# Feature-map attention and two feed-forward stages: the first key block in two transfers, and constants on other queues and places

## The chip, the cores and the metric

The kernel runs on one core of a Trainium2 chip. The metric is the device time of one execution in microseconds (us). Engines are named as in the profile: PE is TensorE, PEld its weight loads, DVE is VectorE, ACT is ScalarE, POOL is GpSimd, SP is SyncE. A name with a q behind it (SPq, ACTq) is that engine's queue of DMA issues.

## The reference

```python
# q, k, v: (4, 8, 576, 64); omega: (128, 64); x = attention output as (2304, 512)
def phi(x):                      # of q * scale and k * scale
    proj = einsum('bhsd,md->bhsm', x, omega)
    h = proj - sum(x * x, -1, keepdims=True) / 2
    return exp(h - max(h, -1, keepdims=True)) / sqrt(m)
kv, z = einsum('bhsm,bhsd->bhmd', phi(k), v), sum(phi(k), 2)
attn = einsum('bhsm,bhmd->bhsd', phi(q), kv) / (einsum('bhsm,bhm->bhs', phi(q), z) + 1e-6)
# then: top-1 mixture of 8 experts (relu, 512 -> 1024 -> 512), gate-weighted,
# then: h = x @ w_in (512 -> 2048), g = piecewise-quadratic relu of h, out = g @ w_out
```

## The kernel before

The program has three stages. The **attention stage** takes the first 172 us; the **expert stage** gathers each expert's tokens and multiplies them by split float32 weights; the **last stage** is the dense layer pair. The last two are nearly back-to-back matmuls on PE.

In the attention stage each head's keys and queries come in blocks of 256 tokens (8 heads, 128 partitions, two tokens to a partition: 512 KB) and in small blocks of the 64 tokens left over in each of two batches. `block_tasks` (L418) makes the work of a block: its load (issued on SP, L432, or L428 for a small one), the squares (ACT for keys, L438; POOL for queries, L440), a tree of two additions on POOL (L445), and a sum on DVE (L449) that gives the squared norm. `unit_tasks` (L465) makes the work of half a block, a unit: four transposes on PE against the identity (L472), a copy on ACT (`th`, L477), 32 small matmuls against omega (`project`, L484), two maxima on DVE (L491), the bias from the maxima and the norm (L495 and L496), and eight exponentials on ACT (L500). The units go k(0,0) first half, the small key block, k(0,1) first half, k(0,0) second half, k(0,1) second half, and then the keys of the next batch and the queries of this one in turn. `kv_tasks`, `c_tasks` and `r_tasks` (L518, L571, L644) come behind: the key-value products, the quotient, and the routing to experts.

Tasks are not run in the order in which they are written. `Plan` (L40) holds them with an engine, a cost in ns, a rank, the tasks they come after and the buffers that they take; `run` picks greedily, by planned start and rank, and then emits all of them in the order of their planned starts. The engines run their own instructions strictly in that order. The planned costs only set the order, never a time on the chip. A load is taken to be usable 2000 ns behind its planned end (`HOPS`, L53). A DMA that is issued outside a task stands in front of all planned work of its engine.

The constants lie in one array of 708 columns: the identity (128 columns, 64 KB), and behind it a triangle of ones, a ramp, token numbers and others (580 columns, 290 KB). The tile is `cs`; the identity is loaded at L191 outside the plan. `omega_tasks` (L382) holds one SP task with three DMAs (omega twice, L387, 32 KB each; the rest of `cs`, L388), the cast of the triangle to bf16 on DVE (`trib`, L397), the transpose of omega on PE (L391), and its scaled copy on ACT (`oms`, L394), which every `project` needs.

The gate's weights are spread into a block matrix by two DVE copies (`gate_blocks`, L413), and four weight tiles of the first expert are loaded and split inside the plan (L281 on POOL, L290 on DVE).

Of the kernel before, what the change touches and what calls it, by code (L numbers as in the profile page):

```python
# [8 lines left out]
F32 = mybir.dt.float32  # L9
# [6 lines left out]
AX = mybir.AxisListType.X  # L16
# [3 lines left out]
P = 128  # L20
B, H, S, HD = 4, 8, 576, 64
# [18 lines left out]
class Plan:  # L40
# [22 lines left out]
    def add(self, engine, cost, fn, rank, after=(), take=(), use=(), mode=None):  # L63
        for b in use:
            b["uses"] += 1
        self.tasks.append((engine, cost, fn, rank, [a for a in after if a is not None], take, use, mode))
        return len(self.tasks) - 1
# [94 lines left out]
def kernel(  # L162
# [14 lines left out]
    nc = tc.nc  # L177
# [10 lines left out]


    cs = cp.tile([P, C_END], F32, name="cs")  # L190
    nc.sync.dma_start(out=cs[:, 0:P], in_=consts[:, 0:P])  # L191
    ident = cs[:, C_ID:C_ID + P]
    trib = cp.tile([P, P], BF16, name="trib")
    oneb = cp.tile([P, P], BF16, name="oneb")
# [129 lines left out]
    with ExitStack() as actx:  # L324
        ap = actx.enter_context(tc.tile_pool(name="ap", bufs=2))
# [19 lines left out]
        add, buf, at = plan.add, plan.buf, plan.tile  # L345
# [33 lines left out]
        om2 = ac.tile([P, 2 * HD], F32, name="om2")  # L379
        oms = ac.tile([P, P], F32, name="oms")  # L380

        def omega_tasks():  # L382
            pb = buf("ps")

            def load():
                for i in range(2):
                    nc.sync.dma_start(out=om2[:, i * HD:(i + 1) * HD], in_=omega)  # L387
                nc.sync.dma_start(out=cs[:, P:C_END], in_=consts[:, P:C_END])  # L388

            def turn():  # L390
                nc.tensor.transpose(at(pb)[:, 0, :], om2, ident)  # L391

            def scaled():
                nc.scalar.activation(oms, at(pb)[:, 0, :], AF.Copy, scale=SCALE)  # L394

            def tri():
                nc.vector.tensor_copy(trib, cs[:, C_TRI:C_TRI + P])  # L397

            x = add("SP", 1300, load, -7.5)
            add("DVE", 130, tri, 1, after=[x])  # L400
            x = add("PE", 110, turn, -5, after=[x], take=[pb], mode="whole")
            return add("ACT", 240, scaled, -5, after=[x], use=[pb])

        wgr = ac.tile([P, 4, E], F32, name="wgr")
# [13 lines left out]
        def block_tasks(which, blk, rank):  # L418
            src = q if which == "q" else k
            small = blk[0] == "s"  # L420
            n = H if small else 2 * H
            o = {"buf": buf("blk")}

            def load():
                t = at(o["buf"])
                if small:
                    for i in range(2):
                        nc.sync.dma_start(out=t[64 * i:64 * i + 64, 0:H, :],  # L428
                                          in_=src[2 * blk[1] + i, :, 512:576, :].rearrange("h p d -> p h d"))
                else:  # L430
                    b, i = blk
                    nc.sync.dma_start(out=t.rearrange("p (h r) d -> p h r d", r=2),  # L432
                                      in_=src[b, :, i * 256:(i + 1) * 256, :].rearrange("h (p r) d -> p h r d", r=2))

            def square(eng):
                raw, t = at(o["buf"])[:, 0:n, :], at(sb)[:, 0:n, :]
                if eng == "ACT":
                    act.activation(t, raw, AF.Square)  # L438
                else:
                    pool.tensor_mul(t, raw, raw)  # L440

            def tree():
                t = at(sb)[:, 0:n, :]
                for w in (32, 16):
                    pool.tensor_add(t[:, :, 0:w], t[:, :, 0:w], t[:, :, w:2 * w])  # L445

            def total():
                o["nsq"] = ap.tile([P, 2 * H], F32, name="nsq", tag="nsq", bufs=12)
                dve.reduce_sum(o["nsq"][:, 0:n], at(sb)[:, 0:n, 0:16], axis=AX)  # L449

            f = 0.5 if small else 1.0
            sb = buf("sqt")
            o["load"] = add("SP", 2250 * f, load, rank - 8, take=[o["buf"]])
            if which == "k":
                t = add("ACT", 950 * f, lambda: square("ACT"), rank - 0.5, after=[o["load"]], take=[sb], use=[o["buf"]])
            else:
                t = add("POOL", 1900 * f, lambda: square("POOL"), rank - 0.5, after=[o["load"]], take=[sb],
                        use=[o["buf"]])
            t = add("POOL", 2000 * f, tree, rank - 0.4, after=[t], use=[sb])
            o["sq"] = add("DVE", 60 + 270 * f, total, rank - 0.3, after=[t], use=[sb])  # L460
            return o

        def unit_tasks(u, o, rank, prev):  # L465
            which, blk, hf = u
            r = {}
# [32 lines left out]
                    act.activation(at(ppb)[:, 2 * j + i, :], at(pjb[i])[:, j, :], AF.Exp, bias=r["bi"][:, i, j:j + 1])  # L500

            pjb = [buf("ps"), buf("ps")]
            ta = add("PE", 435, turn, rank - 1.5, after=[o["load"]] + prev, take=[ptb], use=[o["buf"], ptb], mode="whole")
            x = add("ACT", 480, copy, rank - 2.4, after=[ta], take=[thb], use=[ptb])
            for c in range(4):
                x = add("PE", 220, lambda c=c: project(c), rank + 1 + 0.1 * c, after=[x, setup],
# [1 line left out]
            ends, tb, t = [], x, x  # L508
            for i in range(2):
                t = add("DVE", 600, lambda i=i: top(i), rank + 4.5, after=[t], use=[pjb[i]])  # L510
            t = add("DVE", 150, bias, rank + 1, after=[t, o["sq"]])
            for i in range(2):
                ends.append(add("ACT", 1005, lambda i=i: exps(i), rank + 2, after=[t] + ends[0:1],
                                take=[ppb] if i == 0 else [], use=[pjb[i]]))
# [798 lines left out]
```

## Time and profile before

| | us |
|---|---|
| median of 3 runs | 829.54 (827.75 to 830.61) |
| the profiled execution, its own time | 828.41 |
| its span, first to last instruction | 826.2 |

| engine | busy us | share of the span |
|---|---|---|
| PE | 778.4 | 94% |
| PEld | 710.1 | 86% |
| DVE | 570.1 | 69% |
| POOL | 388.2 | 47% |
| ACT | 366.9 | 44% |

The shares are means over stages with different limits. The time that a change in one stage is worth is read in that stage. The 2.2 us between the profiled execution's own time and its span lie outside the instructions.

### The profile page before, as it was taken

How to read it: one execution, taken by the hardware profiler on the slowest of the kernel's cores; microseconds unless marked ns; L12 is line 12 of the kernel's file. 1: busy time of each engine (PE TensorE's matmuls, PEld its weight loads, DVE VectorE, ACT ScalarE, POOL GpSimd, SP SyncE). 2: the span in 40 equal slices, each digit the busy share in tenths (PEclk: the TensorE clock that was granted, in tenths of full speed). 3: DMA queues.
4: the chain of work that ended last, by engine and by line, in shares of the span. 5: the costliest groups of instructions: out<-in, count | busy, mean ns of one | idle time of the engine just before them, and what ended most of it. 6: DMA issues, size and time to landing. Idle time of an engine off the chain costs nothing.

```text
span 826.2 us, 16881 instructions
## 1 busy us (share of the span) xinstructions
PE 778.4 (94%) x6530; PEld 710.1 (86%) x6530; DVE 570.1 (69%) x1124; ACT 366.9 (44%) x906; POOL 388.2 (47%) x385
## 2 busy tenths in 40 slices
PE   6798799769999999989999999999999999999996
PEld 4687688649999999979998989898999989898985
DVE  5679888865756876475688667687777877745543
ACT  6798799614422222222354554444433443434331
POOL 5627861444446455163655444453434544334333
PEclk9999999969999999999999999999999999999999
DMA  9958301155465655664432001110011100001112
GB/s 224 225 122 210 116 29 28 54 159 177 155 187 177 191 184 186 114 215 144 141 94 80 27 27 47 56 52 27 28 51 51 52 27 1 1 25 52 40 39 81
DMA packets 79034, 80.41 MB, mean 97 GB/s; under 512 B 28972, under 2 KB 61868, under 8 KB 78944
## 3 DMA queue, kind: packets, MB, share of 16 engines
q1 hardware_dynamic: 75056, 68.10, 29.2%
q0 software_dynamic: 3072, 9.57, 3.3%
q10 hardware_dynamic: 816, 1.57, 0.5%
q8 instruction: 53, 0.87, 0.4%
q14 instruction: 37, 0.30, 0.1%
HBM read 69.78 MB, written 9.45 MB: 96 GB/s over the span
## 4 chain that ended last, share of the span: by engine, by line
PE 71%; DVE 11%; DMA 8%; ACT 4%; issue 3%; POOL 2%; POOLq 0%; SPq 0%; DVEq 0%
PE ph L1117 7%; PE ph L1118 7%; PE ph L1119 7%; PE po L1163 7%; PE po L1162 7%; PE po L1161 7%; DMA out_dram<-acc,oidx 5%; PE py L1031 4%; PE py L1033 3%; PE py L1032 3%; PE ph L1013 3%; PE ph L1014 3%; PE ph L1015 3%; ACT pp L500 3%; DMA wraw<-in_moe_w_dram 2%
## 5 line engine op out<-in xcount | busy, mean ns | idle before, releaser
L1146 POOL TENSOR_TENSOR gl<-cl,gh 128x384 fp32r<-128x384 f32 x94 | 99.5, 1078 | 186.5 <-ACT gh L1145 186.5
L1138 ACT ACTIVATE cl<-cl,half 128x384 f32<-128x384 f32 x96 | 57.0, 615 | 212.4 <-DVE cl L1137 212.4
L1117 PE MATMUL ph<-yh,wh 128*128 128x384 f32 x384 | 129.8, 338 | 0.0
L1118 PE MATMUL ph<-yl,wh 128*128 128x384 f32 x384 | 129.7, 338 | 0.0
L1119 PE MATMUL ph<-yh,wl 128*128 128x384 f32 x384 | 129.7, 338 | 0.0
L281 POOL TENSOR_SCALAR wh<-wraw 128x1024 fp32r<-128x1024 f32 x60 | 75.0, 1252 | 111.9 <-DMA wraw<-in_moe_w_dram 46.8
L1163 PE MATMUL po<-wh,gl 128*128 128x512 f32 x288 | 113.9, 395 | 0.0
L1162 PE MATMUL po<-wl,gh 128*128 128x512 f32 x288 | 113.7, 395 | 0.0
L1161 PE MATMUL po<-wh,gh 128*128 128x512 f32 x288 | 113.6, 394 | 0.0
L1137 DVE TENSOR_SCALAR cl<-ph 128x384 f32<-128x384 f32 x96 | 51.4, 552 | 81.9 <-PE ph L1119 81.1
L290 DVE TENSOR_TENSOR wl<-wraw,wh 128x1024 fp32r<-128x1024 f32 x60 | 77.3, 1288 | 16.3 <-POOL wh L281 16.3
L500 ACT ACTIVATE pp<-ps,bi 128x128 f32<-128x128 f32 x288 | 84.3, 478 | 6.4 <-DVE bi L496 6.4
L937 DVE TENSOR_TENSOR yl<-yT,yh 128x384 fp32r<-128x384 f32 x96 | 79.0, 880 | 8.9 <-ACT yh L936 8.9
L1013 PE MATMUL ph<-xh,wh 128*128 128x288 f32 (+6 forms) x256 | 78.8, 308 | 3.0 <-DVE hl L1019 2.6
L1031 PE MATMUL py<-hh,wh 128*128 128x288 f32 (+6 forms) x256 | 79.1, 309 | 0.0
L1014 PE MATMUL ph<-xl,wh 128*128 128x288 f32 (+6 forms) x256 | 77.2, 302 | 1.1 <-DVE xl L975 1.0
L1032 PE MATMUL py<-hl,wh 128*128 128x288 f32 (+6 forms) x256 | 76.6, 299 | 0.7 <-DVE hl L1019 0.5
L1015 PE MATMUL ph<-xh,wl 128*128 128x288 f32 (+6 forms) x256 | 77.1, 301 | 0.0
L1033 PE MATMUL py<-hh,wl 128*128 128x288 f32 (+6 forms) x256 | 76.6, 299 | 0.4 <-DVE wl L290 0.4
L1117 PEld LDWEIGHTS ph<-yh,wh 128*128 128x128 f32 x384 | 72.1, 188 | 2.1
L1118 PEld LDWEIGHTS ph<-yl,wh 128*128 128x128 f32 x384 | 72.1, 188 | 2.0
L1119 PEld LDWEIGHTS ph<-yh,wl 128*128 128x128 f32 x384 | 72.1, 188 | 0.0
(163 smaller groups left out, 1664.6 us busy)
## 6 DMA issues: line engine op xcount, KB each, us to landing
wraw<-in_moe_w_dram SPq DMA_DIRECT2D x57, 512.0 KB, 3.8
wraw<-in_moe_w_in_dram SPq DMA_DIRECT2D x16, 512.0 KB, 3.9
wraw<-in_moe_w_out_dram SPq DMA_DIRECT2D x16, 512.0 KB, 3.4
blk<-in_k_dram SPq DMA_DIRECT2D x8, 512.0 KB, 6.6
blk<-in_q_dram SPq DMA_DIRECT2D x8, 512.0 KB, 6.1
vm<-in_v_dram SPq DMA_DIRECT2D x16, 256.0 KB, 5.3
xd<-xr SPq DMA_DIRECT2D x16, 256.0 KB, 2.2
wra<-in_moe_w_dram SPq DMA_DIRECT2D x4, 512.0 KB, 7.0
```

The lines of the kernel that those rows point to most:

```text
L500: act.activation(at(ppb)[:, 2 * j + i, :], at(pjb[i])[:, j, :], AF.Exp, bias=r["bi"][:, i, j:j + 1])
L1013: nc.tensor.matmul(ph, lhsT=wh[:, d, c], rhs=xh, start=(d == 0), stop=False)
L1014: nc.tensor.matmul(ph, lhsT=wh[:, d, c], rhs=xl, start=False, stop=False)
L1015: nc.tensor.matmul(ph, lhsT=wl[:, d, c], rhs=xh, start=False, stop=(d == 3))
L1031: nc.tensor.matmul(py, lhsT=wh[:, a, c], rhs=hh, start=(f == 0), stop=False)
L1032: nc.tensor.matmul(py, lhsT=wh[:, a, c], rhs=hl, start=False, stop=False)
L1117: nc.tensor.matmul(ph[f], lhsT=wh[:, a, c], rhs=yh, start=(d == 0), stop=False)
L1118: nc.tensor.matmul(ph[f], lhsT=wh[:, a, c], rhs=yl, start=False, stop=False)
L1119: nc.tensor.matmul(ph[f], lhsT=wl[:, a, c], rhs=yh, start=False, stop=(d == 3))
L1161: nc.tensor.matmul(po, lhsT=gh[:, c], rhs=wh[:, a, :], start=(f == 0), stop=False)
L1162: nc.tensor.matmul(po, lhsT=gh[:, c], rhs=wl[:, a, :], start=False, stop=False)
L1163: nc.tensor.matmul(po, lhsT=gl[:, c], rhs=wh[:, a, :], start=False, stop=(f == 3))
```

## The change

The identity is loaded on ACT's queue in place of SP's. The two omega transfers leave the SP task and are issued on ACT's queue ahead of the plan, behind the identity. The SP task of `omega_tasks` keeps only the 290 KB of other constants; its planned cost goes from 1300 to 600 and its rank from -7.5 to -5.5, and the transpose of omega no longer comes after it. The loads of k(0,0), the small key block and k(0,1) have the ranks -8, -7 and -6. The block k(0,0) alone gets two loads of four heads each (ranks -8 and -7.8), and its squares, tree and sum are made by half; each unit waits only for its own half. All other blocks keep one part.

```diff
-    nc.sync.dma_start(out=cs[:, 0:P], in_=consts[:, 0:P])
+    nc.scalar.dma_start(out=cs[:, 0:P], in_=consts[:, 0:P])
...
+            for i in range(2):
+                nc.scalar.dma_start(out=om2[:, i * HD:(i + 1) * HD], in_=omega)
+
             def load():
-                for i in range(2):
-                    nc.sync.dma_start(out=om2[:, i * HD:(i + 1) * HD], in_=omega)
                 nc.sync.dma_start(out=cs[:, P:C_END], in_=consts[:, P:C_END])
...
-            x = add("SP", 1300, load, -7.5)
+            x = add("SP", 600, load, -5.5)
             add("DVE", 130, tri, 1, after=[x])
-            x = add("PE", 110, turn, -5, after=[x], take=[pb], mode="whole")
+            x = add("PE", 110, turn, -5, take=[pb], mode="whole")
...
+            parts = 2 if which == "k" and blk == (0, 0) else 1
+            w = n // parts
...
+                    h = H // parts
+                    nc.sync.dma_start(out=t[:, i * w:(i + 1) * w, :].rearrange("p (h r) d -> p h r d", r=2),
+                                      in_=src[b, i * h:(i + 1) * h, j * 256:(j + 1) * 256, :].rearrange(
+                                          "h (p r) d -> p h r d", r=2))
...
-            f = 0.5 if small else 1.0
+            f = w / 16
             sb = buf("sqt")
+            o["load"], o["sq"] = [], []
+            for i in range(parts):
+                o["load"].append(add("SP", 2250 * f, lambda i=i: load(i), rank - 8 + 0.2 * i, take=[] if i else [o["buf"]]))
+            for i in range(parts):
+                if which == "k":
+                    t = add("ACT", 950 * f, lambda i=i: square("ACT", i), rank - 0.5, after=o["load"][i:i + 1],
+                            take=[] if i else [sb], use=[o["buf"]])
...
+                t = add("POOL", 2000 * f, lambda i=i: tree(i), rank - 0.4, after=[t], use=[sb])
+                o["sq"].append(add("DVE", 60 + 270 * f, lambda i=i: total(i), rank - 0.3, after=[t] + o["sq"], use=[sb]))
...
-            ta = add("PE", 435, turn, rank - 1.5, after=[o["load"]] + prev, take=[ptb], use=[o["buf"], ptb], mode="whole")
+            ta = add("PE", 435, turn, rank - 1.5, after=[o["load"][hf % len(o["load"])]] + prev, take=[ptb], use=[o["buf"], ptb], mode="whole")
...
-            t = add("DVE", 150, bias, rank + 1, after=[t, o["sq"]])
+            t = add("DVE", 150, bias, rank + 1, after=[t, o["sq"][hf % len(o["sq"])]])
```

## Rows read from the trace of the kernel before

**Rows 1.** Busy time by stage: us, PE, PEld, DVE, ACT, POOL, granted clock, DMA share, GB/s.

```profile
17.00:25.00 8.00, 6.06 (x117) 4.61 (x112) 7.90 (x16) 8.00 (x27) 3.97 (x4) 1.00 1.08 202
60.00:80.00 20.00, 16.74 (x312) 14.46 (x306) 18.84 (x55) 16.57 (x54) 14.40 (x17) 0.91 0.86 220
186.00:800.00 614.00, 609.34 (x3556) 565.42 (x3555) 416.42 (x631) 225.99 (x468) 282.77 (x246) 1.00 0.29 89
```

**Rows 2.** The chain of waits from 0 to 40 us: start, us, what.

```profile
1.18 4.22 DMA blk<-in_k_dram
...
5.53 1.10 PE ps L472 x4
...
6.65 0.60 ACT th L477
7.25 0.18 ACT oms L394
...
7.47 1.99 PE ps L484 x32
...
32.68 2.15 issue
```

**Rows 3.** Timeline of the first 8 us: start, us, engine, line, what, idle before.

```profile
0.73 0.39 SPq L191 DMA_DIRECT2D cs<-in_consts_dram  x1
0.74 1.28 ACT L438 ACT_TABLE_LOAD   x1 [0.74 <-PEq L1296]
...
1.64 1.05 SPq L387 DMA_DIRECT2D om<-in_omega_dram  x2
...
3.21 1.41 SPq L428 DMA_DIRECT2D blk<-in_k_dram  x2
...
6.41 0.42 PE L391 MATMUL ps<-cs,om 128*128 128x128 f32 x1
...
7.05 0.84 DVE L397 CAST trib<-cs 128x128 bf16<-128x128 f32 x1 [6.04 <-DMA cs<-in_consts_dram]
```

**Rows 4.** DMA throughput from 0 to 5 us, in 40 equal slices.

```profile
GB/s 0 0 0 0 0 0 0 0 0 0 0 0 0 12 25 152 250 74 78 111 123 164 152 78 168 184 274 356 336 348 352 348 326 328 371 314 296 331 272 179
```

**Rows 5.** DMA issues: engine, count, size of each, us from issue to landing.

```profile
xd<-xr SPq DMA_DIRECT2D x16, 256.0 KB, 2.2
...
cs<-in_consts_dram SPq DMA_DIRECT2D x1, 290.0 KB, 4.3
...
blk<-in_k_dram SPq DMA_DIRECT2D x2, 128.0 KB, 4.7
```

**Rows 6.** The timeline where ACT's queue issues a DMA, at 180 us.

```profile
180.84 0.43 ACTq L232 DMA_DIRECT2D wraw<-in_moe_w_dram  x1
```

**Rows 7.** The timeline of the small key block, whose rows have half a block's size.

```profile
9.03 0.63 ACT L438 ACTIVATE sqt<-blk 128x512 f32<-128x512 f32 x1 [1.61 <-DMA blk<-in_k_dram]
...
9.74 1.25 POOL L445 TENSOR_TENSOR sqt<-sqt 128x256 f32<-128x256 f32 x2 [1.13 <-ACT sqt L438]
...
11.03 0.29 DVE L449 TENSOR_REDUCE nsq<-sqt 128x8 f32<-128x128 f32 x1 [0.83 <-POOL sqt L445]
11.19 1.98 PE L484 MATMUL ps<-oms,th 64*64 64x128 f32 x32 [0.69 <-ACT th L477]
```

**Rows 8.** The timeline: the first use of the other constants.

```profile
60.94 0.18 DVE L664 SCALAR_TENSOR_TENSOR req<-rd,cs 128x16 f32<-128x16 f32 x1
```

**Rows 9.** The timeline around PE's stall at 32.7 us.

```profile
32.00 2.63 ACT L500 ACTIVATE pp<-ps,bi 128x128 f32<-128x128 f32 x8
...
33.11 2.30 DVE L413 COPY wgb<-wgr 64x32 f32<-64x32 f32 x2
...
37.30 0.60 ACT L477 ACTIVATE th<-ps 128x512 f32<-128x512 f32 x1 [2.67 <-PE ps L472]
```

**Rows 10.** Busy time behind that stall, columns as in rows 1.

```profile
35.00:36.00 1.00, 1.00 (x18) 0.67 (x15) 0.97 (x2) 0.00 (x0) 0.92 (x2) 0.53 1.00 215
...
38.00:39.00 1.00, 1.00 (x8) 0.92 (x7) 0.76 (x3) 0.38 (x1) 0.92 (x2) 0.76 0.73 163
```

More of the change, by code (lines that the diff above doesn't have):

```diff
@@ L422, in block_tasks, with load, square @@
             o = {"buf": buf("blk")}
-            def load():
+            parts = 2 if which == "k" and blk == (0, 0) else 1
+            w = n // parts
+            def load(i):
                 t = at(o["buf"])
                 if small:
-                    for i in range(2):
-                        nc.sync.dma_start(out=t[64 * i:64 * i + 64, 0:H, :],
-                                          in_=src[2 * blk[1] + i, :, 512:576, :].rearrange("h p d -> p h d"))
-                else:
[L431 to L436, printed above, removed]
+                    for j in range(2):
+                        nc.sync.dma_start(out=t[64 * j:64 * j + 64, 0:H, :],
+                                          in_=src[2 * blk[1] + j, :, 512:576, :].rearrange("h p d -> p h d"))
+                else:
+                    b, j = blk
+                    h = H // parts
+                    nc.sync.dma_start(out=t[:, i * w:(i + 1) * w, :].rearrange("p (h r) d -> p h r d", r=2),
+                                      in_=src[b, i * h:(i + 1) * h, j * 256:(j + 1) * 256, :].rearrange(
+                                          "h (p r) d -> p h r d", r=2))
+            def square(eng, i):
+                raw, t = at(o["buf"])[:, i * w:(i + 1) * w, :], at(sb)[:, i * w:(i + 1) * w, :]
                 if eng == "ACT":
@@ L440, in square @@
                     pool.tensor_mul(t, raw, raw)
[L442 to L449, printed above, removed]
-            f = 0.5 if small else 1.0
-            sb = buf("sqt")
-            o["load"] = add("SP", 2250 * f, load, rank - 8, take=[o["buf"]])
@@ L454, in block_tasks, with tree @@
[L454 to L460, printed above, removed]
+            def tree(i):
+                t = at(sb)[:, i * w:(i + 1) * w, :]
+                for c in (32, 16):
+                    pool.tensor_add(t[:, :, 0:c], t[:, :, 0:c], t[:, :, c:2 * c])
@@ new lines, in total @@
+            def total(i):
+                if i == 0:
+                    o["nsq"] = ap.tile([P, 2 * H], F32, name="nsq", tag="nsq", bufs=12)
+                dve.reduce_sum(o["nsq"][:, i * w:(i + 1) * w], at(sb)[:, i * w:(i + 1) * w, 0:16], axis=AX)
+            f = w / 16
+            sb = buf("sqt")
+            o["load"], o["sq"] = [], []
+            for i in range(parts):
+                o["load"].append(add("SP", 2250 * f, lambda i=i: load(i), rank - 8 + 0.2 * i, take=[] if i else [o["buf"]]))
@@ new lines, in block_tasks @@
+            for i in range(parts):
+                if which == "k":
+                    t = add("ACT", 950 * f, lambda i=i: square("ACT", i), rank - 0.5, after=o["load"][i:i + 1],
+                            take=[] if i else [sb], use=[o["buf"]])
+                else:
+                    t = add("POOL", 1900 * f, lambda i=i: square("POOL", i), rank - 0.5, after=o["load"][i:i + 1],
+                            take=[sb], use=[o["buf"]])
+                t = add("POOL", 2000 * f, lambda i=i: tree(i), rank - 0.4, after=[t], use=[sb])
+                o["sq"].append(add("DVE", 60 + 270 * f, lambda i=i: total(i), rank - 0.3, after=[t] + o["sq"], use=[sb]))
```

## The prediction

> **What bounds the kernel now.** I read four views in this order. First busy time by stage. From 186 to 800 us PE is busy 609 of 614 us at a granted clock of 1.00 [rows 1]: whatever the attention stage gives back, this block only starts earlier by as much, and nothing in it can swallow or add to the gain. So the question is when the attention stage ends. Within that stage no single engine is full all the time: ACT is busy 8.00 of 8 us from 17 to 25, DVE has 18.84 of 20 from 60 to 80 [rows 1]. It is a fixed order of tasks over four engines, where now one and now another is waited for.
>
> Then the chain of waits for the first 40 us [rows 2]. It begins with one transfer, the first key block: issued at 1.18, landed 4.22 us later. Behind it stand four transposes (1.10), the copy `th` (0.60), the copy `oms` (0.18) and the first projection at 7.47. From 17 us on ACT has no idle time [rows 1]. The timeline [rows 3] shows why the head is as it is: SP issues the identity at 0.73 (0.39 us) and so k(0,0) only behind it, omega comes after (1.64, two issues in 1.05 us), then the other constants, and the small key block only at 3.21. The last view is DMA throughput [rows 4]: nothing moves until 1.6 us, then the identity, then some 110 to 160 GB/s until 3.1, and from 3.3 on around 340 GB/s. The head is latency of issue and transfer, not work.
>
> **The change part by part.** *The first half of k(0,0).* Its issue moves up to where the identity's was, 0.73 in place of 1.18: 0.45 us. It waits for 256 KB less; at the 340 GB/s of the last stretch [rows 4] that is 0.26 MB / 340 GB/s = 0.77 us. So it lands at about 5.40 - 0.45 - 0.77 = 4.2 us. The bound on the early side is the issue at 0.73 with the 2.2 us that a 256 KB transfer takes from issue to landing at a quieter time [rows 5], 2.9; on the late side the 4.7 us that 128 KB transfers in this crowd take [rows 5], 5.4. I take 4.2, since it comes from the very transfer that is cut.
>
> *Identity and omega on ACT's queue.* The trace has ACT's queue issue a DMA in 0.43 us [rows 6]. Three of them, from 0.74, the time of ACT's first instruction [rows 3], end at 2.0; omega's second goes out at 1.6. The table load (1.28 us) [rows 3] goes behind them, 2.0 to 3.3, and costs nothing as long as ACT's first work is not before 3.3; if it came first, the three issues would be 1.28 us later (that is in a rival below). When omega lands the trace doesn't show, only that it had landed by the matmul at 6.41, which stood in line behind the transposes [rows 3]. Bounds: 1.6 + 2.2 = 3.8 and 1.6 + 4.3 = 5.9 (the other constants' 290 KB took 4.3 [rows 5]). I take 4.2, near the low end: omega is 32 KB, and the crowd of [rows 4] is not there yet when it goes out.
>
> A rule bears on this. The Trainium skill (DMA: Bandwidth & Descriptors, Issuing engines are not separate DMA queues) says that transfers from several engines run on the same 16 DMA engines and that a second issuer saves only the sequencer's issue time. By that the move is worth the 0.39 + 1.05 us of SP's issue time and no bandwidth, and the halves of k(0,0) share with omega; the 128 KB of both constants at that rate is under 0.4 us, which lies inside the bounds. The same page (Rules for kernel authors) speaks against cutting the transfer: at least 1 MiB each, since each pays a fixed cost of about 2 us. By that the second half would land up to 2 us later than now; no row here has such a pair.
>
> The second half is needed only by the fourth unit, whose transposes come around 13 us; it goes out at about 1.2, so even 5.9 us to land are covered five us deep. I cost it at nothing.
>
> *The order on PE and ACT.* Omega's transpose now comes after no load and so is planned first on PE, ahead of the key transposes; `oms` is first on ACT. That is a new wait: the transposes of k(0,0), and with them everything, are queued behind omega's landing. With both at 4.2: omega's transpose 4.3 to 4.7 (0.42 [rows 3], half of it beside the next weight load), the four key transposes until 5.7 (1.10), `th` 0.60 until 6.3, projection at 6.35. Before it was 7.47: **1.1 us earlier**. `oms` (0.18 to 0.27) and the half squares (0.63 [rows 7]) fit on ACT before 5.7. With omega at 3.8 the projection is at 6.05, 1.4 us earlier; with omega at 5.9 it is at 5.9 + 0.25 + 1.1 + 0.6 + 0.1 = 7.95, 0.5 us later.
>
> *Squares and sums by half.* Two squares of half a block cost 2 x 0.63 on ACT, two trees 2 x 1.25 on POOL, two sums 2 x 0.29 on DVE [rows 7], in place of one of each at twice the size. What is added on an engine is at most one of the two, 0.63, 1.25 and 0.29 us, and falls before 11 us, where ACT waits 1.61 and DVE 0.83 us in these very rows [rows 7]; and the first half's norm is ready sooner than the whole was. Nothing on the path.
>
> *The small block and k(0,1).* SP reaches the small block at about 1.65, 3.21 before [rows 3]; its square waited for its landing at 9.03 [rows 7]. At 1.6 us earlier it lands at 7.4, while PE is busy with the first projection until 6.35 + 1.99 = 8.35. So the second unit starts behind the first without a wait, and its projection, at 11.19 before [rows 7], comes at about 10.1. k(0,1) and the rest follow on the same queue with the same bytes ahead of them or fewer. The gain is kept to where ACT's exponentials become the chain.
>
> *The other constants behind three blocks.* They go out at about 3.6 to 5 and land, by the 4.3 and 4.7 us of [rows 5], between 7.9 and 9.7. The columns of `cs` are first read at 60.94 [rows 8]: 50 us of cover. But the cast `trib`, which now starts at 7.05 after 6.04 us of waiting for that load [rows 3], waits for it on DVE, and maxima are queued behind it. By ranks and planned starts it comes behind the first maximum of the second unit, which can't start before that projection's end at 10.1 + 2.0, so the latest landing of 9.7 is covered by 2.4 us. If that cover were gone, each us late would be a us late for the second unit's bias and exponentials.
>
> **Sum.** Head -1.1 us, the rest nothing: the profiled 828.41 (span 826.2 and 2.2 around it) becomes 827.3. The profiled execution lies 1.1 below the median of the runs, so for the median 829.54 - 1.1 = **828.4**. A measurement of this kernel can tell some 0.3%, 2.5 us, from no change, so by itself this is no measurable change.
>
> **The unknown that is larger than the sum.** The change alters planned starts unevenly: SP's later tasks by 0.7 us (1300 to 600), those that hang on the first block by more. The planner is greedy, so tasks of the whole attention stage may come in another order. What one such place is worth the trace shows. At 32.68 PE stands for 2.15 us in the chain [rows 2], while ACT works off eight exponentials until 34.6 and DVE spends 2.30 us in `gate_blocks` [rows 9]; ACT then waits 2.67 us for PE's transposes. Behind the stall PE's granted clock is 0.53 in the first and 0.76 in the last of four slices of 1 us [rows 10], so mostly at the lower of its two levels (1.2 of 2.4 GHz); with the two between taken as the first, 3 x 0.47 + 0.24 = 1.6 us are lost. Price of one such place: 2.15 + 1.6 = 3.7 us.
>
> **Rivals.** *(A) The head gains nothing.* Either omega lands near 5.5, or the table load stays first on ACT and puts identity and omega 1.28 us later (4.2 + 1.28 = 5.5): then transposes to 6.85, projection at 7.55, 0.1 later than now: 829.6. For it: the transfers' landing is unseen, and PE now waits for omega first. Against: the first bytes move 0.9 us after the identity's issue ends [rows 3, 4]. A rule stands on this side of it: the Trainium skill (ScalarE: Activation LUTs, ACT is a hardware spline evaluator) has the table load placed right before the activation that needs it, so behind the issues; the row shows it first because there nothing stands ahead of it.
>
> *(B) The new order is without the stall at 32.7 us.* -1.1 - 3.7 = -4.8: 824.7. For it: the stall hangs on where `gate_blocks`, the exponentials and two POOL tasks happen to meet, and the compute tasks move against SP's. Against: PE waits there for ACT, which is full from 32.0 to 34.6 in any order near this one.
>
> *(C) The new order has one more such stall*, in the DVE-bound part where little slack is left (60 to 80 us [rows 1]) or around 25 us: -1.1 + 3.7 = +2.6: 832.1. It decides from the point where a task that waits is put ahead of a maximum or a bias on DVE for over 1.1 us, the head's gain.
>
> That the change doesn't do what it says I leave out: the order of loads on SP follows from the ranks alone.
>
> **How the numbers follow.** Forecast (head gain carried, order equal in worth) 0.55, with its own range of 826.5 to 830.5 (head between -1.4 and +0.5, and the runs' own spread); A 0.13; B 0.19; C 0.13. B is given more than C since a place is already in the trace that can be removed. Faster by over 2.5 us (under 827.0): B whole and a sixth of the forecast, 0.28. Slower by over 2.5 us: most of C, 0.12. Within: 0.60. The range reaches from B's 824.7 to just short of C, 831.6, and leaves out about a fifth: C, and the edges of B and of the forecast.
>
> **What would show it.** Right: the first key transposes near 4.5 and the projection near 6.35 with omega's transpose ahead; the small block's square without a wait for its load; `trib` with no wait that matters; the exponentials of the first units 1.1 earlier, and the end of the attention stage too. Wrong: PE's first instruction waiting for omega or the identity beyond 4.7; another order of DVE's tasks after 25 us with a new or a missing stall; a shift at the end of the stage that isn't the one at 15 us. The first would be A, the others B or C.

## The result

The changed kernel takes 834.26 us in the median of 7 runs (831.88 to 837.18), the kernel before 828.37 beside it (7 runs, 824.15 to 830.61). The ratio on record is 1.0092, with a 95% interval of [1.0068, 1.0115]: slower by 0.9%, and the time is outside the range that was predicted. (This ratio is not the quotient of the two medians, which is 1.0071; the two measures lie up to some 0.2% apart in what follows, so the loss is 5.9 us by the medians and 7.6 by the ratio.) The profiled execution of the changed kernel has a time of 831.88 and a span of 829.8; against 828.41 and 826.2 before, it shows 3.5 of the 5.9 us by which the medians differ. The first part of its page, busy time of each engine, share of the span and instructions, is nearly that of the kernel before:

```profile
PE 778.1 (94%) x6530; PEld 708.7 (85%) x6530; DVE 568.5 (69%) x1125; ACT 367.0 (44%) x907; POOL 386.5 (47%) x387
```

The work is the same to within 2 us on each engine; what came is waiting.

**The head.** The chain of waits of the changed kernel from 0 to 12 us (start, us, what):

```profile
1.68 3.83 DMA om<-in_omega_dram
...
6.09 0.87 PE ps L484 x4
...
7.63 1.98 PE ps L496 x32
```

The chain no longer begins with the key block but with omega, on ACT's queue: it lands at 5.51, and the transposes of the keys stand behind omega's. The first projection comes at 7.63, 0.16 later than before [rows 2], where 1.1 earlier was forecast. Lines of the timeline of the same kernel, up to 14 us (start, us, engine, line, what; in brackets the idle time before):

```profile
0.73 1.02 SPq L438 DMA_DIRECT2D blk<-in_k_dram  x2
0.74 0.43 ACTq L191 DMA_DIRECT2D cs<-in_consts_dram  x1
1.20 0.93 ACTq L386 DMA_DIRECT2D om<-in_omega_dram  x2
2.16 1.28 ACT L395 ACT_TABLE_LOAD   x1 [2.16 <-issue]
...
5.65 0.45 PE L392 MATMUL ps<-cs,om 128*128 128x128 f32 x1 [5.65 <-DMA om<-in_omega_dram]
...
7.48 1.14 ACT L445 ACTIVATE sqt<-blk 128x512 f32<-128x512 f32 x2
...
13.99 0.22 DVE L398 CAST trib<-cs 128x128 bf16<-128x128 f32 x1
```

The issues are where they were expected, the table load is behind them, the second half's square runs at 7.48 without a wait, with the small block's behind it, and the cast `trib` waits for nothing. Only omega is late, and by the chain everything waits for it.

**The stage.** Busy time of the kernel before, by a stretch (us, PE, PEld, DVE, ACT, POOL, granted clock, DMA share, GB/s):

```profile
17.00:27.00 10.00, 8.06 (x162) 6.28 (x158) 9.79 (x21) 10.00 (x35) 3.97 (x4) 1.00 1.01 188
```

and of the changed kernel:

```profile
17.00:27.00 10.00, 6.08 (x117) 4.42 (x110) 8.39 (x16) 8.47 (x28) 6.63 (x6) 1.00 1.10 187
...
186.00:800.00 614.00, 609.29 (x3553) 565.75 (x3552) 414.53 (x632) 226.88 (x470) 279.81 (x245) 1.00 0.30 90
```

Before, ACT was full from 17 us on; now it has 1.53 us of idle time between 17 and 27, and PE does 1.98 us less, at a clock of 1.00 in both. Behind the attention stage the block is as rigid as it was [rows 1]. The end of the attention stage is read from the first gather of the expert stage, in the timeline of before and then of after:

```profile
174.37 1.16 POOL L963 DMA_INDIRECT xg<-xd,gidx  x1 [3.64 <-DVE u L889]
```

```profile
176.53 1.16 POOL L975 DMA_INDIRECT xg<-xd,gidx  x1 [3.71 <-DVE u L901]
```

So 2.2 of the 3.6 us of span are lost before the gather, and 0.2 of these in the head. (The other 1.4 come behind the gather, in work that the change doesn't touch; there a stretch of this execution was granted less clock, see the end.)

**What stands differently.** ACT's order between 7 and 24 us. Before, the square of k(0,1) ran in ACT's idle time, ahead of the first unit's first four exponentials:

```profile
11.04 1.05 ACT L438 ACTIVATE sqt<-blk 128x1024 f32<-128x1024 f32 x1
12.35 1.14 ACT L500 ACTIVATE pp<-ps,bi 128x128 f32<-128x128 f32 x4 [0.26 <-DVE bi L496]
```

After, it comes behind those four and behind the copies `th` of the next two units, for which ACT waits:

```profile
11.65 1.14 ACT L512 ACTIVATE pp<-ps,bi 128x128 f32<-128x128 f32 x4 [0.36 <-DVE bi L508]
14.41 0.60 ACT L489 ACTIVATE th<-ps 128x512 f32<-128x512 f32 x1 [1.62 <-PE ps L484]
15.26 0.60 ACT L489 ACTIVATE th<-ps 128x512 f32<-128x512 f32 x1 [0.26 <-PE ps L484]
15.76 1.05 ACT L445 ACTIVATE sqt<-blk 128x1024 f32<-128x1024 f32 x1
...
16.88 2.07 POOL L452 TENSOR_TENSOR sqt<-sqt 128x512 f32<-128x512 f32 x2 [6.19 <-ACT sqt L445]
...
18.91 1.89 POOL L447 TENSOR_TENSOR sqt<-blk 128x1024 f32<-128x1024 f32 x1
...
19.47 0.41 DVE L457 TENSOR_REDUCE nsq<-sqt 128x16 f32<-128x256 f32 x1
...
19.80 1.03 DVE L507 SCALAR_TENSOR_TENSOR mx<-nsq,mx 128x8 f32<-128x8 f32 x1
...
20.89 2.07 POOL L452 TENSOR_TENSOR sqt<-sqt 128x512 f32<-128x512 f32 x2
20.95 1.23 DVE L507 SCALAR_TENSOR_TENSOR mx<-nsq,mx 128x8 f32<-128x8 f32 x1
...
22.41 1.14 ACT L512 ACTIVATE pp<-ps,bi 128x128 f32<-128x128 f32 x4 [1.53 <-DVE bi L508]
```

The square is 4.7 us later than before. Its tree leaves POOL idle for 6.19 us, so POOL's work behind it is late as well, and the exponentials at 22.41 us wait 1.53 us for their bias. That wait is not simply the late norm. The sum is done at 19.9 and DVE didn't wait for the tree; but the two corrections of the maxima behind the sum (L507) take 1.03 and 1.23 us, while POOL multiplies and adds, and in the trace each ends within 0.03 us of a POOL instruction (20.81 and 22.15). Where the square is moved back (below), POOL is idle at this point, and the same two corrections take 0.15 and 0.16 us:

```profile
19.98 0.41 DVE L459 TENSOR_REDUCE nsq<-sqt 128x16 f32<-128x256 f32 x1
...
20.31 0.15 DVE L512 SCALAR_TENSOR_TENSOR mx<-nsq,mx 128x8 f32<-128x8 f32 x1
...
20.58 0.16 DVE L512 SCALAR_TENSOR_TENSOR mx<-nsq,mx 128x8 f32<-128x8 f32 x1
```

There the sum is even 0.5 us later than here, and yet the exponentials come at 20.97. Together the two corrections take 1.9 us more in the changed kernel than there, and the wait is 1.53 us: as far as these two traces show, it comes from POOL's work, which has slid over DVE's corrections.

The tasks are the same; the planner put them in another order. In its planned times, worked out from the kernel's own costs, k(0,1) was usable at 7625 ns and the four exponentials were ready at 7595: the exponentials went first by 30 ns of plan.

### The profile page after: what moved, and what is told of

The parts are those of the page before. It is cut to its first block, busy times and chain, and to the rows that moved or that the text cites. A ratio compares the mean times of both kernels' runs of the same rounds, so it can differ in the third digit from the quotient of the medians.

```text
span 829.8 us, 16885 instructions
## 1 busy us (share of the span) xinstructions
PE 778.1 (94%) x6530; PEld 708.7 (85%) x6530; DVE 568.5 (69%) x1125; ACT 367.0 (44%) x907; POOL 386.5 (47%) x387
## 4 chain that ended last, share of the span: by engine, by line
PE 70%; DVE 13%; DMA 8%; issue 3%; ACT 3%; POOL 2%; POOLq 0%; ACTq 0%; DVEq 0%
PE ph L1129 7%; PE ph L1131 7%; PE ph L1130 7%; PE po L1175 7%; PE po L1174 7%; PE po L1173 7%; DMA out_dram<-acc,oidx 5%; PE py L1043 4%; PE py L1044 3%; PE py L1045 3%; PE ph L1025 3%; PE ph L1026 3%; PE ph L1027 3%; DVE mx L503 3%; PE ps L496 2%
## 5 line engine op out<-in xcount | busy, mean ns | idle before, releaser
L1158 POOL TENSOR_TENSOR gl<-cl,gh 128x384 fp32r<-128x384 f32 x94 | 102.8, 1114 | 186.9 <-ACT gh L1157 186.9
L281 POOL TENSOR_SCALAR wh<-wraw 128x1024 fp32r<-128x1024 f32 x60 | 70.5, 1176 | 118.5 <-DMA wraw<-in_moe_w_dram 61.0
```

The costliest lines, as they stand in the source:

```text
L1158: rest.tensor_sub(gl, cl, gh.bitcast(F32))
```

## The experiments

Each ratio is the one on record, against runs of the kernel before made beside it, with its 95% interval. One count serves as a measure of progress: the exponentials of the units done by 27 us. It is the line of the exponentials alone, from 0 to 27 us (us, ACT's busy time and, in brackets, the count, then clock, DMA share, GB/s); before:

```profile
0.00:27.00 27.00, 10.56 (x38) 1.00 0.99 213
```

and after:

```profile
0.00:27.00 27.00, 7.52 (x27) 1.00 1.08 219
```

### The transfers without the order, and the order without the transfers

*New transfers, old order.* All tasks keep the order of before; only the transfers are the new ones, and the parts by half are issued inside the old tasks.

```diff
-    nc.sync.dma_start(out=cs[:, 0:P], in_=consts[:, 0:P])
+    nc.scalar.dma_start(out=cs[:, 0:P], in_=consts[:, 0:P])
...
+            for i in range(2):
+                nc.scalar.dma_start(out=om2[:, i * HD:(i + 1) * HD], in_=omega)
...
+            parts = 2 if which == "k" and blk == (0, 0) else 1
+            cut = [slice(g * n // parts, (g + 1) * n // parts) for g in range(parts)]
...
+            def load_late():
+                load()
+                nc.sync.dma_start(out=cs[:, P:C_END], in_=consts[:, P:C_END])
```

> All transfers of the change (identity and omega on ACT's queue, k(0,0) in two loads with halved squares, trees and sums, the other constants behind k(0,1) with the cast trib behind the second unit's first maximum), but every other task in the order of the kernel before, omega's transpose behind the first key transposes among them. Order theory (the loss is the new order of tasks): as the kernel before or up to 1.1 us faster, ratio 0.997 to 1.001; the first projection near 6.4 us, where 7.47 was before. Transfer theory (the loss is that omega lands at 5.5 us on a second ring and the two rings slow each other): as the changed kernel, ratio about 1.009.

Measured: 828.64 us, ratio 0.9995 [0.9971, 1.0019]. Two lines of its timeline:

```profile
4.24 1.09 PE L486 MATMUL ps<-cs,blk 128*128 128x128 f32 x4 [4.24 <-DMA blk<-in_k_dram]
...
6.58 1.99 PE L498 MATMUL ps<-oms,th 64*64 64x128 f32 x32 [0.52 <-ACT oms L395]
```

With the keys ahead of omega on PE the transposes start at 4.24. The projection, behind the copies `th` and `oms`, comes at 6.58: 0.9 earlier than before. In the trace the gain is carried: by 27 us this kernel has 40 exponentials done, and its first gather is at 173.66, 0.7 earlier. In the time it can't be told from nothing. The transfers are not the loss.

*Old transfers, new order.* The tasks stand as in the changed kernel; the loads go out as before. The edit is against the changed kernel.

```diff
-    nc.scalar.dma_start(out=cs[:, 0:P], in_=consts[:, 0:P])
+    nc.sync.dma_start(out=cs[:, 0:P], in_=consts[:, 0:P])
...
-            for i in range(2):
-                nc.scalar.dma_start(out=om2[:, i * HD:(i + 1) * HD], in_=omega)
-
             def load():
-                nc.sync.dma_start(out=cs[:, P:C_END], in_=consts[:, P:C_END])
+                pass
...
+                    if parts == 2:
+                        return
...
+        first = plan.tiles["blk"][0]
+        nc.sync.dma_start(out=first.rearrange("p (h r) d -> p h r d", r=2),
+                          in_=k[0, :, 0:256, :].rearrange("h (p r) d -> p h r d", r=2))
+        for i in range(2):
+            nc.sync.dma_start(out=om2[:, i * HD:(i + 1) * HD], in_=omega)
+        nc.sync.dma_start(out=cs[:, P:C_END], in_=consts[:, P:C_END])
```

> All transfers of the kernel before (everything on SP's queue, k(0,0) in one load, the other constants ahead of the small block), but all compute tasks in the order of the changed kernel. Order theory: as slow as the changed kernel, ratio 1.006 to 1.012. Transfer theory: as the kernel before, ratio 0.998 to 1.002.

Measured: 833.28 us, ratio 1.0050 [1.0028, 1.0071]; 24 exponentials by 27 us, first gather at 177.44. The order alone loses, with the first projection at 7.92, 0.45 us later than before. Its 0.5% is below the 0.6 to 1.2% that was expected, but inside the interval of the changed kernel's second measurement below.

*Another order by one number.* The kernel before with the planned cost of the SP task of `omega_tasks` at 600 in place of 1300. No instruction and no transfer is another; only the order is.

```diff
-            x = add("SP", 1300, load, -7.5)
+            x = add("SP", 600, load, -7.5)
```

> The kernel before with one number changed, the planned cost of omega's SP task, 1300 to 600 as in the change; the same instructions and transfers, but the planner's order differs from the kernel before about as much as the changed kernel's does. Order theory: the time moves by some us, in a direction that can't be told ahead; a ratio off 1 by 0.003 to 0.01 either way. Transfer theory: 0.997 to 1.003, since no transfer is touched.

Measured: 834.69 us, ratio 1.0080 [1.0050, 1.0111]. It has 27 exponentials by 27 us. Lines of its timeline:

```profile
8.68 1.09 PE L472 MATMUL ps<-cs,blk 128*128 128x128 f32 x4 [1.88 <-DMA blk<-in_k_dram]
...
9.70 3.58 PE L484 MATMUL ps<-oms,th 64*64 64x128 f32 x64
...
180.68 1.16 POOL L963 DMA_INDIRECT xg<-xd,gidx  x1 [3.64 <-DVE u L889]
```

One planned number, which stands for no time on the chip, costs about as much as the whole change. But the order that it draws is not the changed kernel's: here PE takes the transposes of the small key block ahead of the first projection and waits 1.88 us for that block, so the projection is 2.2 us late at 9.70 already. This run shows what a redrawn order can cost with nothing else touched; that the changed kernel's own order is its loss is shown by the two runs above.

### Omega

*One omega transfer.* The changed kernel with omega loaded once; DVE copies the second half. The order is the changed kernel's.

```diff
-            for i in range(2):
-                nc.scalar.dma_start(out=om2[:, i * HD:(i + 1) * HD], in_=omega)
+            nc.scalar.dma_start(out=om2[:, 0:HD], in_=omega)
+            nc.vector.tensor_copy(om2[:, HD:2 * HD], om2[:, 0:HD])
```

> The changed kernel with one omega transfer and a copy on DVE for the second half, same order of tasks. Omega's first transfer landed at 4.34 us in the changed kernel, the second at 5.51, so omega's transpose should start near 4.75 in place of 5.65 and the first projection near 6.8 in place of 7.63. Order theory: still slower than before, ratio 1.004 to 1.010. Transfer theory (late omega is the loss): ratio 0.998 to 1.001.

Measured: 833.20 us, ratio 1.0050 [1.0024, 1.0076]. Two lines of its timeline:

```profile
4.74 0.48 PE L392 MATMUL ps<-cs,om 128*128 128x128 f32 x1 [4.74 <-DVE om L386]
...
6.75 1.98 PE L496 MATMUL ps<-oms,th 64*64 64x128 f32 x32 [0.69 <-ACT th L489]
```

The one transfer has landed, and its copy is made, by 4.74; of the two it was the second that came at 5.51. The projection is 0.9 us earlier than in the changed kernel, and so is the first gather, at 175.63. That is what omega's second transfer cost in the trace; in the ratio it can't be told from the noise, and most of the loss stays.

*The same with the order of before,* on top of the new transfers; the second half's square and tree come behind `oms`.

```diff
+            nc.scalar.dma_start(out=om2[:, 0:HD], in_=omega)
+            nc.vector.tensor_copy(om2[:, HD:2 * HD], om2[:, 0:HD])
...
+            def rest():
+                t = at(sb)[:, cut[1], :]
+                act.activation(t, at(o["buf"])[:, cut[1], :], AF.Square)
```

> The new transfers in the order of the kernel before, with one omega transfer (the second half is copied on DVE) and the second half of k(0,0)'s square and tree behind the copies th and oms, so that nothing of the second half stands ahead of the first projection. Order theory: projection near 6.2 us (7.47 before, 6.58 in the first run of this series), 1.2 us earlier all through the attention stage; ratio 0.997 to 1.000, faster than both kernels by what can hardly be measured. Transfer theory: as the changed kernel less about 1 us, 1.004 to 1.008.

Measured: 828.23 us, ratio 0.9988 [0.9964, 1.0012]. Again no difference that can be told, as with two omega transfers in the old order.

### The place in the order

*Square first.* The changed kernel; only k(0,1)'s square goes back ahead of the first unit's exponentials.

```diff
+                if blk == (0, 1) and which == "k" and o.pop("moved", False):
+                    return
...
+                if u == ("k", (0, 0), 0) and i == 0:
+                    ahead_of[0]["square"]("ACT", 0)
+                    ahead_of[0]["moved"] = True
```

> The changed kernel with one ACT instruction moved: the square of k(0,1) goes ahead of the first unit's exponentials again, where the kernel before has it, in place of behind two copies; all else in the changed kernel's order. In the changed kernel that square ran at 15.8 us (11.0 before) and the exponentials were 2.9 us behind the kernel before at 27 us. Flip theory (this one swap is the loss): the exponentials at 27 us at most 0.8 us behind the kernel before, the end of the attention stage within 0.5 us of it, ratio 0.999 to 1.003. Spread theory (the new order loses at many places, and the swap's loss is partly given back by 45 us anyway): better at 27 us, but the end of the stage still 1.5 us or more behind, ratio 1.004 to 1.009.

*The changed kernel again,* beside it, without an edit.

> The changed kernel itself once more, beside the others of this call on the same chip. Both theories: 1.005 to 1.010; it is the measure for the one above.

Measured: 831.33 us, 1.0013 [0.9990, 1.0035], with the square moved back, and 833.32, 1.0061 [1.0036, 1.0086], for the changed kernel. With the square back there are 33 exponentials by 27 us, against 26 in the changed kernel's second profile. One instruction's place gives back 2.0 of 3.8 us by the medians, and 4.0 of 5.1 by the ratios (0.48% of 829.5); the two intervals lie just side by side, so that it helps is fairly sure and how much is not. The traces don't show the gain at the end: with the square back, the kernel has 100 exponentials by 60 us (103 in the changed kernel), and its gather, at 178.31, is later than the changed kernel's 177.25. That execution, at 833.84, lies 2.5 us above the median of its own runs, so the gain rests on the medians alone, and the end of the stage within 0.5 us of the kernel before, which was expected if this swap were the whole loss, was not seen.

*Square late, alone.* The opposite way: the kernel before, and only this square and its tree go behind the first unit's exponentials and the two copies.

```diff
+                if blk == (0, 1) and which == "k" and not moved:
+                    moved.append(lambda: square(eng))
+                    return
...
+                if u == ("k", (0, 0), 1):
+                    for fn in list(moved):
+                        fn()
```

> The kernel before with the one swap of the changed kernel put in: k(0,1)'s square on ACT stands behind the first unit's first exponentials and the copies of the next two units, all else as before. Flip theory (this swap is most of the loss): exponentials 1.5 to 3 us late at 27 us and not given back, ratio 1.002 to 1.006. Spread theory: late at 27 us, but given back by the end of the stage, ratio 0.998 to 1.002.

Measured: 831.73 us, ratio 1.0027 [1.0005, 1.0048]. Lines of its timeline:

```profile
15.39 1.05 ACT L441 ACTIVATE sqt<-blk 128x1024 f32<-128x1024 f32 x1
...
18.62 0.42 DVE L455 TENSOR_REDUCE nsq<-sqt 128x16 f32<-128x256 f32 x1 [3.92 <-POOL sqt L451]
...
20.67 1.10 PE L493 MATMUL ps<-oms,th 64*64 64x128 f32 x32 [2.49 <-ACT th L483]
```

It has 33 exponentials by 27 us. DVE, which has the sum ahead of other work, stands 3.92 us for the tree; PE stands 2.49 us for a copy that queues behind on ACT; the first gather, at 176.37, comes 2.0 us later than before. The loss is 2.2 us (0.27% of 829), with an interval from 0.4 to 4.0. It is not the same loss as in the changed kernel: the sum keeps its old place on DVE here and is waited for, which in the changed kernel it isn't. So the late square costs some 2 us or more by either way, but each size is known only within a few us.

### Other orders

*Planned cost 900.* The edit of the cost-600 kernel, with 900.

```diff
-            x = add("SP", 1300, load, -7.5)
+            x = add("SP", 900, load, -7.5)
```

> The kernel before with the planned cost of omega's SP task at 900 in place of 1300, the same instructions and transfers; another redraw of the order. Order theory: a time that differs from the kernel before by some us, likelier slower, as 600 was by 0.8%: ratio 1.002 to 1.010. If the order before is nothing special, the ratio should as well lie below 1.

Measured: 827.49 us, ratio 0.9988 [0.9967, 1.0010]. Two numbers, 600 and 900, give two orders that are 7 us apart in the median. A slower kernel was expected here (1.002 to 1.010); 900 is not.

*The order of 900 with the new transfers and one omega.*

```diff
+            nc.scalar.dma_start(out=om2[:, 0:HD], in_=omega)
+            nc.vector.tensor_copy(om2[:, HD:2 * HD], om2[:, 0:HD])
...
-            x = add("SP", 1300, load, -7.5)
+            x = add("SP", 900, load, -7.5)
```

> The order that a planned cost of 900 gave (0.9988 before), with the transfers of the change, one omega transfer and the second half's square behind the copies (0.9988 in the old order). Order theory: both gains are independent, so 0.996 to 0.999, about 2 us faster than the kernel before and than the changed kernel by some 6. If the head gain is swallowed, as the kernel before: 0.999 to 1.001.

Measured: 824.67 us in the median of 9 runs, ratio 0.9954 [0.9927, 0.9980]. One of the runs, the profiled one, took 4211 us and shows nothing; the ratio leaves it out, and the kernel ran once more:

> The last kernel but two once more, since its profiled execution there was disturbed and shows nothing: the order of planned cost 900 with the transfers of the change, one omega transfer and the second half's square behind the copies. Order theory: 0.994 to 0.998; first projection near 6.2 us, exponentials at 27 us some 2 us ahead of the kernel before. If the earlier gain was chance: 0.998 to 1.001.

Measured: 825.92 us over 12 runs, ratio 0.9969 [0.9942, 0.9995]. It has 40 exponentials by 27 us. Two lines of its timeline:

```profile
6.53 1.98 PE L508 MATMUL ps<-oms,th 64*64 64x128 f32 x32 [0.37 <-ACT oms L395]
...
170.20 1.16 POOL L990 DMA_INDIRECT xg<-xd,gidx  x1 [3.64 <-DVE u L916]
```

Both measurements of it lie below 1: with the transfers of the change, one of omega among them, in an order that suits them, the kernel is faster than the kernel before by 0.3 to 0.5%, and so than the changed one. How much of this is the transfers and how much the order of 900 can't be told: the intervals of this kernel and of the order of 900 alone overlap.

*The planner is told of omega.* The changed kernel, where omega's transpose comes after a task that does nothing and ends so that omega counts as usable at 5500 ns, its measured landing.

```diff
+            "ACTQ": dict.fromkeys(("PE", "ACT", "DVE", "POOL", "SP"), 2000.0)}
...
-            x = add("PE", 110, turn, -5, take=[pb], mode="whole")
+            y = add("ACTQ", 3500, lambda: None, -8)
+            x = add("PE", 110, turn, -5, after=[y], take=[pb], mode="whole")
```

> The changed kernel, but the planner takes omega as usable at 5500 ns, which is where it lands on the chip, in place of 0; this draws the order anew. If the loss comes from that wrong belief alone: ratio 0.998 to 1.002. If an order that is drawn anew is simply another draw, the ratio can be anything from 0.996 to 1.010, and this run alone doesn't tell a good belief from a good draw unless it is slow.

Measured: 831.22 us, ratio 1.0029 [1.0006, 1.0053]; first gather at 176.10. Lines of its timeline:

```profile
6.92 1.09 PE L486 MATMUL ps<-cs,blk 128*128 128x128 f32 x4 [1.40 <-DMA blk<-in_k_dram]
...
8.87 0.49 PE L498 MATMUL ps<-oms,th 64*64 64x128 f32 x4 [0.64 <-ACT oms L396]
```

With the true landing in the plan the first keys go ahead of omega's transpose, but so do those of the small block, which land at 6.8: the first projection comes 1.2 us later than in the changed kernel. Yet the gather is 0.4 us earlier, and the ratio, taken at another time, lower than either of the changed kernel's two. The ratio lies above the 0.998 to 1.002 that was expected if the wrong landing in the plan were the whole loss. The head doesn't decide; what the order does behind it does.

*All kernels side by side.* Exponentials by 27 and by 60 us, start of the first projection and of the first gather (us, from one profiled execution each), and the ratio:

| kernel | 27 us | 60 us | projection | gather | ratio |
|---|---|---|---|---|---|
| before | 38 | 104 | 7.47 | 174.37 | 1 |
| changed | 27 | 103 | 7.63 | 176.53 | 1.0092 |
| changed, again | 26 | 103 | 7.83 | 177.25 | 1.0061 |
| new transfers, old order | 40 | 105 | 6.58 | 173.66 | 0.9995 |
| old transfers, new order | 24 | 100 | 7.92 | 177.44 | 1.0050 |
| cost 600 | 27 | 105 | 9.70 | 180.68 | 1.0080 |
| one omega | 31 | 104 | 6.75 | 175.63 | 1.0050 |
| one omega, old order | 40 | 104 | 6.39 | 174.15 | 0.9988 |
| square first | 33 | 100 | 7.61 | 178.31 | 1.0013 |
| square late, alone | 33 | 104 | 7.26 | 176.37 | 1.0027 |
| cost 900 | 40 | 111 | 7.40 | 171.03 | 0.9988 |
| cost 900, new transfers | 40 | 112 | 6.53 | 170.20 | 0.9969 |
| omega known | 35 | 104 | 8.87 | 176.10 | 1.0029 |

The kernels with 38 and more exponentials by 27 us have the ratios up to 1, those with fewer the ratios above it. But the count is of one kind of task, and it isn't kept: by 60 us most kernels stand within a few of each other. It tells good orders from bad ones here; it doesn't tell where the time is lost for good.

## Why the prediction was wrong

**The first half of k(0,0): right.** Its landing was put at 4.2; in the four kernels in which PE takes it first, the transposes start between 4.12 and 4.44 (4.24 in the one shown).

**Omega: the mechanism right, the size wrong.** The prediction saw that everything would be queued behind omega, took 4.2 from bounds of 3.8 to 5.9, and named the rival in which it lands near 5.5 and the projection comes at 7.55. Its second transfer landed at 5.51, the projection came at 7.63. So the head's term was +0.16 and not -1.1. Of the two causes given for that rival it is not the table load, which ran behind the issues as forecast. It is the transfer itself: in flight from 1.68 on, it took 3.83 us for 32 KB. By the trace's semaphore events, omega's two transfers and the two halves of k(0,0) landed in the order of their issue, though on two queues: the first half at 4.13, omega's first at 4.34, the second half at 5.23, omega's second at 5.51. The bound on the low side came from a transfer in a quiet time [rows 5], and this one had both halves of k(0,0) issued ahead of it; the value should have been taken near the high end. (No run has omega without the key block beside it, so that the block is the reason is read and not tested.)

The trace agrees with the rule that was weighed there. The Trainium skill (DMA: Bandwidth & Descriptors, Issuing engines are not separate DMA queues) says that a second issuing engine saves only sequencer time. Omega's second transfer was issued about 0.6 us earlier than before (1.68 against 2.26), and by the semaphore events it landed 0.3 us earlier, 5.51 against 5.82; the first, which now has half a key block ahead of it in place of a whole one, gained 1.3 (4.34 against 5.61).

**Halves, the small block, the other constants: right.** The squares by half ran at 6.30 and 7.48, and the second half had landed at 5.23, where the whole block had landed at 5.39; the up to 2 us more that were weighed for it didn't appear. By the semaphore events the small block landed at 6.85, earlier than the forecast 7.4, and the other constants at 9.34, inside 7.9 to 9.7; `trib` at 13.99 stood far behind that. By the transfers the forecast holds as a whole: with the old order they move the head by -0.9 and the time by nothing that can be told.

**"Order equal in worth": the step that failed.** The prediction named the redrawn order as an unknown larger than its sum, then gave the forecast 0.55 on the case that it cancels out, and 0.19 to a better order against 0.13 to a worse one. The order was worse: the old transfers in it lose 0.5% (4.1 us of 829), while the new transfers in the old order give 0.9995. A term that the forecast put at zero was most of the loss. Rival C had the sign and the stretch ("around 25 us") and, nearly, its condition, a bias that is held up on DVE: the exponentials at 22.41 us waited 1.53 us for theirs, not behind a task that waits, but because the two corrections ahead of it took 1.03 and 1.23 us beside POOL. Its price was taken from PE's stall with the lost clock behind it, while from 17 to 27 us the granted clock is 1.00: the loss there is ACT's and PE's plain waiting. That C's 832.1 us comes near the 834.26 is in part luck.

**Rival B's stall did go, and its gain went into the loss ahead of it.** In the changed kernel PE doesn't stand at 32.7 us any more; its timeline shows 0.24 us where there had been 2.15 [rows 2], with `gate_blocks` beside it as before [rows 9]:

```profile
34.61 2.53 DVE L414 COPY wgb<-wgr 64x32 f32<-64x32 f32 x2
34.75 1.75 PE L496 MATMUL ps<-oms,th 64*64 64x128 f32 x54 [0.24 <-ACT pp L512]
```

The gain doesn't reach the gather: by 27 us the kernel was 11 exponentials behind, and it only caught up, to 1 behind by 60 us. Where one looks for a stall that may go, the order moves others in.

**Two readings in the prediction are off,** without a term that hangs on them. The first bytes move 0.5 us after the identity's issue ends (1.12 and about 1.63 [rows 3, 4]), not 0.9, which is the time from its start; and the slices between 2.1 and 3.1 us have 74 to 168 GB/s, not 110 to 160.

**What stays open.** That the order is the loss, or most of it, is shown. Where in it the time is lost is shown in part: the square's place costs some 2 us or more, known within a few us, and omega's landing 0.9 us in the head and at the gather of one trace. The loss was 5.9 us by the medians in the first comparison and 3.8 in the second. The rest lies in the order as well, since the old transfers in that order lose 0.5%, but no single place of it was singled out. The stretches behind 60 us don't settle it; the kernel before, the changed kernel, and the changed kernel's second profile:

```profile
60.00:100.00 40.00, 31.51 (x627) 27.49 (x622) 36.07 (x112) 30.62 (x98) 31.37 (x37) 0.91 0.62 163
100.00:140.00 40.00, 36.93 (x858) 33.13 (x857) 33.55 (x111) 37.35 (x125) 18.72 (x24) 1.00 0.08 28
```

```profile
60.00:100.00 40.00, 32.92 (x698) 28.42 (x697) 39.24 (x118) 34.34 (x110) 29.00 (x34) 1.00 0.60 157
100.00:140.00 40.00, 34.73 (x807) 31.19 (x807) 33.26 (x108) 33.22 (x112) 17.41 (x24) 0.96 0.08 29
```

```profile
60.00:100.00 40.00, 32.57 (x673) 28.80 (x672) 38.37 (x108) 32.25 (x102) 27.96 (x33) 0.93 0.59 157
100.00:140.00 40.00, 35.30 (x829) 31.66 (x828) 34.17 (x110) 35.08 (x118) 18.31 (x23) 0.98 0.08 29
```

In the first profile the changed kernel does more of ACT's work from 60 to 100 us (34.34 against 30.62) and 4.1 us less from 100 to 140; in its second profile both differences are about half as large. The granted clock goes the same way (0.91, 1.00 and 0.93 in the first stretch; 1.00, 0.96 and 0.98 in the second), so these stretches can't be told from the clock's own differences between executions.

## What to carry to other kernels

Where a planner draws the order of the instructions, every planned cost, rank or dependence that an edit touches redraws all of it, and orders with the very same instructions lay 0.9% apart here: test the edit with the order held fixed, and then draw the order anew as a change of its own. Cost such a redrawing as a spread to both sides, not at zero, and look first at the places where the plan decides by a few tens of ns, as between this square and the exponentials (30 ns). Look also at what such a move slides over: here POOL's late work fell on DVE's corrections. When a small transfer is put at the head of everything, take its landing from the transfers issued ahead of it, and plan with that time.

## What the runs showed of the hardware

A 32 KB transfer took 3.83 us from issue to landing though ACT's queue had only the identity and the other copy of omega on it: with a queue of its own it still landed behind the half key block that SP had issued 0.45 us earlier (5.51 and 5.23). A DVE instruction on 128x8 elements, some 0.16 us long otherwise, took 1.03 and 1.23 us beside POOL's work and ended within 0.03 us of a POOL instruction; in the attention stage of the kernel before, 12 of the 18 such corrections and biases that start during a POOL addition or multiplication take over 0.4 us, of the 54 others 2. And the runs of one kernel spread by some 5 to 10 us (the kernel before in one comparison: 824.58 to 834.50 over 30 runs) with a granted clock that falls at other places in other executions. The clock of the page, 40 slices of the span, in two profiled executions of the changed kernel:

```profile
PEclk9999999959999999999999999999999999999999
```

```profile
PEclk9999899959999999999999999999999999999999
```

The instructions are the same, yet the fifth slice is at 9 in the first and at 8 in the second. In the first the granted clock is also lower in a stretch that ran at 1.00 in the kernel before, and it is there that the 1.4 us behind the gather begin:

```profile
360.00:370.00 10.00, 7.42 (x39) 6.92 (x38) 7.55 (x9) 1.33 (x3) 6.08 (x5) 0.85 0.67 210
```

So a difference under some 3 us is not read from one pair of traces; the medians of many runs tell it.
